# Fixed task lists for five engines, w_in loaded once and copied on chip, and q and k in four chunks, in a fused attention and gated-MLP block

## The chip, the core and the metric

The kernel runs on one core of a Trainium2 chip. The core's engines run side by side, each through its own list of instructions in order, and wait for each other only through semaphores: TensorE (PE in the profile, its weight loads PEld), VectorE (DVE), ScalarE (ACT), GpSimd (POOL) and SyncE (SP), which here issues transfers alone. The metric is the time of one execution in microseconds (us) on the device.

## What is computed

The input is 2048 tokens of width 448, in bf16. First comes attention with 16 heads of 28, in which each token sees itself and seven earlier ones at a distance of two, then an MLP whose gate is mixed over all tokens by a 2048 x 2048 matrix. Cut to its core:

```python
def _A_ref(x, wqkv, wo):               # S = 2048, D = 448, H = 16, Dh = 28
    W, dil = (8, 2)
    qkv = (x @ wqkv).reshape(B, S, 3, H, Dh).transpose(2, 0, 3, 1, 4)
    q, k, v = (qkv[0], qkv[1], qkv[2])
    idx = pos[:, None] - (jnp.arange(W) * dil)[None, :]
    mask = idx >= 0
    logits = jnp.einsum('bhsd,bhswd->bhsw', q, kg) * Dh ** (-0.5)   # kg, vg: k, v at idx
    attn = _softmax(jnp.where(mask, logits, -1e9), axis=-1)
    o = jnp.einsum('bhsw,bhswd->bhsd', attn, vg)
    return o.transpose(0, 2, 1, 3).reshape(B, S, D) @ wo

def _B_ref(x, w_in, w_sp, b_sp, w_out):   # Fh = 896
    z = _gelu(x @ w_in)
    z1 = z[..., :Fh]
    z2 = _layernorm(z[..., Fh:])
    g = jnp.einsum('ts,bsf->btf', w_sp, z2) + b_sp[None, :, None]
    return (z1 * g) @ w_out

h = x + _A_ref(_layernorm(x), A_wqkv, A_wo)
out = h + _B_ref(_layernorm(h), B_w_in, B_w_sp, B_b_sp, B_w_out)
```

## The kernel before

**Tiling.** The tokens are cut into two halves of 1024 (the streams, s = 0 and 1), which lie in the two halves of the 128 partitions of `xh`, `qT` and `kT`, so that one pair of matmuls with 64 rows each works on both at once. A *unit* u is 128 tokens of each stream (blocks u and u + 8 of `x_tm`); there are eight. An attention *tile* i is 114 tokens of each stream; there are nine. 14 tokens ahead of the second stream (the halo, `xhalo`) are normalized apart.

**Stages.** For each unit: statistics on DVE (`bn1_*`), the reciprocal root on POOL (`rs1_*`, function `rstd`), normalization on DVE (`nrm1_*`), and the transpose into `xh`, by TensorE for units 0 to 2 (`tT1_*`, evicted by `ev1_*`) and by a transposing transfer on SP for units 3 to 7 (`tD1_*`). The weights of q, k and v land in 64 partitions, and copies (`cpq*`, `cpk*`, `cpv10`) bring them to both halves. q and k are made in chunks of tokens (`mmq*`, `mmk*`, L791, evicted by `evq*`, `evk*`), three chunks with borders 0, 128, 512, 1024 for q. Each tile then takes v (`mmv`, L831), logits (`mml`, L866, 64 small matmuls), Exp on ACT (`exp`, L879), a band mask on DVE (`mask`, L886), row sums (`mmr`, L895), Ln and Exp on ACT for the reciprocal (`ln`, `rex`, L903 and L925), outputs (`mmo`, L915, 64 small matmuls) and their scaling on DVE (`ot`, L933). For each unit follow the projection (`mmy`, L969), the residual sum (`h`, L977), the second normalization and transposing transfer (`tD2_*`), and the gated half of w_in (`mmz2`, L989) with Gelu on ACT (`ge`) and its own normalization. Then come the other half (`mmz1`, L1033, Gelu `gz1`), the token mixing (`g`, L1070, 448 matmuls of 512 columns, evicted by `ua` and `um` on DVE) and the last projection (L1099, `oa`, stores `st`).

**What sets the order.** The kernel is written as some 650 tasks with an engine, a duration, dependencies, and claims on pools (eight PSUM banks, rings of buffers). `Planner.run` simulates the engines and, whenever one is free, gives it the ready task of the lowest priority number. Priorities come from a due time per tile (`t_tile`) and the offsets in `OFF`, with random noise from `SEED`. The task's instructions are emitted when it is picked, so that the order of picking is the order of the instructions on each engine. `Sched.issue` turns reads and writes of buffers into semaphore waits. A dependency that touches no buffer orders the simulation only; where a transfer must in fact wait, it stands in `waits`.

**Warm-up.** `c_warm` (L616) fills the tile `warm` on DVE. Once its task has ended, the planner fills a gap that it foresees on TensorE with matmuls of `warm` by `warm` (`fill`, L633), whose results nobody reads.

**Transfers.** x comes by `ld_x` (L576), the weights of q, k, v by `ld_w` (L583), w_in by `ld_win` (L591): each half of its columns is read twice from memory, once for each half of the partitions, on ACT's queue. w_sp comes in 32 transposing transfers on SP (`ld_wsp`, L950), 16 for each half of the output tokens; in each chain one waits until the one before it has landed. All of SP's instructions are in one line, so that a transfer that waits holds the ones behind it.

**Instructions.** TensorE's credit (`QUEUE`, `ISSUE`, `pe_time`) stands for instructions that wait ahead of it: small matmuls cost at least 31 ns each once the credit is used up.

Of the kernel before, what the change touches and what calls it, by code (L numbers as in the profile page):

```python
# [36 lines left out]
MPEN = 68.974  # L37
OFF = {"q": -480.93, "v": 1236.52, "evv": 825.88, "l": -1029.33, "exp": 175.61, "mask": -1046.78, "r": -491.23, "o":
       -1335.49, "ln": 982.35, "ot": 136.39, "y": -146.01, "h": 162.89, "ln2": 571.73, "z2": 105.24, "ge": 2308.87,
       "n3": 1032.57, "x0": -505.85, "xd": 734.44, "evq": 1025.79, "cp": 119.01, "td": 182.58}  # L40
SEED, SIGMA = 242706, 1.0
O_AFTER_LN = True
NBANKS = 8
TU = 29.85
# [128 lines left out]
class Task:  # L173
    __slots__ = ("name", "eng", "dur", "emit", "deps", "prio", "acq", "rel", "mode", "epoch",
                 "gate", "nbytes", "start", "end", "succ", "ndep", "rt", "nmm", "alts", "bw", "waits", "mark")

    def __init__(self, name, eng, dur, emit, deps=(), prio=0.0, acq=(), rel=(), mode=None,
# [14 lines left out]
        self.bw = 215.0  # L192
        self.waits = []
# [8 lines left out]
class Planner:  # L202
# [4 lines left out]
    def __init__(self, pools, epochs, table_task, marker):  # L207
        self.tasks = []
        self.named = {}
        self.filler = None  # L210
        self.marker = marker
        self.rng = random.Random(SEED)
        self.pools = {k: [(0.0, s) for s in v] for k, v in pools.items()}
        self.epochs = epochs
        self.table_task = table_task

    def add(self, *a, **k):
        t = Task(*a, **k)
        if SIGMA and not t.nbytes:
            t.prio += self.rng.gauss(0.0, SIGMA)  # L220
# [21 lines left out]
    QUEUE = 90  # L242
    FILL = (0.5, 0.3, 0.25)
    ISSUE = 0.031
    SWITCH = 0.1

    def pe_time(self, t, credit):

        return max(t.dur, (t.nmm - credit) * self.ISSUE)

    def run(self, setup=2.0, t0=0.7):
        import heapq
        tasks = self.tasks
        for t in tasks:
            for d in t.deps:
                d.succ.append(t)
            t.ndep = len(t.deps)
# [17 lines left out]
        credit, credit_at = float(self.QUEUE), 0.0  # L275
# [5 lines left out]
        while ndone < len(tasks):  # L281
# [22 lines left out]
            while progress:  # L304
                progress = False
                for e in self.ENGS:
# [3 lines left out]
                    cr = min(self.QUEUE, credit + (now - credit_at) / self.ISSUE)  # L310

                    def key(t):
                        if e != "pe":
                            return t.prio
                        return t.prio + (MPEN if t.mode != pe_mode else 0.0) + WPEN * (self.pe_time(t, cr) - t.dur)
                    best = None
                    for t in sorted(ready[e], key=key):
                        if t.rt > now + 1e-9:
                            continue
                        if t.epoch is not None and t.epoch > cur:  # L320
# [22 lines left out]
                    if t.epoch is not None:  # L343
                        want = self.epochs[t.epoch]
                        if loaded != want:
                            self.table_task(want)
                            loaded = want
                            extra += 1.3
                        left[t.epoch] -= 1
# [4 lines left out]
                    if e == "pe":  # L354
                        dur = self.pe_time(t, cr)
# [3 lines left out]
                        credit = max(0.0, cr - t.nmm + (dur + extra) / self.ISSUE)  # L359
                        credit_at = now + dur + extra  # L360
                        credit = min(credit, self.QUEUE)
                    if e == "pe" and self.filler is not None and self.pools["ps"]:
                        tf, bank = min(self.pools["ps"])
                        room = now - max(free["pe"], tf + 0.3, self.filler[0].end + 0.2) - self.FILL[1]
                        if room > self.FILL[0]:
                            self.filler[1](bank, int(room / self.FILL[2]) + 1)
# [3 lines left out]
                    if t.nbytes:  # L370
                        beg = max(dma_free, now + 0.3)
                        dma_free = beg + t.nbytes / t.bw / 1000.0
                        t.end = dma_free + setup
# [18 lines left out]
def bass_sequential_preLN__sliding_local_dilated__mixer_gmlp__prompt_kernel(  # L392
# [18 lines left out]
    with contextlib.ExitStack() as top:  # L411
# [25 lines left out]
        nhalf = sb("nhalf", [128, 2], F32)  # L437
        st1 = sb("st1", [128, NB, 6], F32)
# [54 lines left out]
        r_win = [[Res("w_in%d_%d" % (z, s)) for s in range(2)] for z in range(2)]  # L493
        r_q = [[Res("q%d_%d" % (c, g)) for g in range(4)] for c in range(3)]
        r_k = [[Res("k%d_%d" % (c, g)) for g in range(4)] for c in range(3)]
# [17 lines left out]
        r_nhalf = Res("nhalf")  # L513
        r_ln1 = [Res("ln1_%d" % b) for b in range(NB)]
# [41 lines left out]
        def dma(eng, name, fn, nbytes, deps=(), prio=0.0, reads=(), writes=(), rel=(), store=False, issue=0.5, bw=245.0, after=()):  # L556
# [13 lines left out]
            t.bw = bw  # L570
            return t
# [15 lines left out]
        t_win = {}  # L587

        def ld_win(z, prio):
# [17 lines left out]
        t_x[2].deps.append(t_x[8])  # L607
        t_x[2].waits.append(t_x[8])
# [8 lines left out]
        cst("c_nhalf", [(lambda e: e.memset(nhalf[:], -0.5), [], [r_nhalf])], 0.1, prio=-99.5)  # L617
# [30 lines left out]
        def ln_unit(u, which, src_deps, prio, ev_deps):  # L648
# [8 lines left out]

            def em_r():
                rr = [rl[bl[0]], rl[bl[1]]]
                rstd(rs[:, u:u + 9:8], mv[:, u:u + 9:8, 1], nhalf[:, 0:2], rr)  # L660
            tr = add("rs%d_%d" % (which, u), "pool", 1.1, em_r, deps=tb, prio=prio)
# [9 lines left out]
            if u in DMA_T[which]:  # L671
# [3 lines left out]
                    rel=[("tr", h)], issue=1.3)  # L675
# [20 lines left out]
        for u in range(NU):  # L696
            t_xh.append(ln_unit(u, 1, [t_x[u], t_x[u + 8]], OFF["x0"] + OFF["xd"] * u, ()))
            if u == 0:
# [6 lines left out]
                th = add("rsh", "pool", 1.05, lambda: rstd(rsh[:, :], mvh[:, 1:2], nhalf[0:16, 0:1], [r_lnh]), deps=[th], prio=2.2)  # L705
# [45 lines left out]
        for n, (p, h, j) in enumerate([("q", h, j) for j in range(2) for h in range(2)] +  # L751
# [4 lines left out]
            def em(p=p, h=h, j=j, tk=tk):  # L756
                if p == "v":
                    copy(tk[0].eng, wv[64:128], wv[0:64], [r_st[p]], [r_w[p][1]])
                else:
# [3 lines left out]
                    prio=OFF["cp"] + 0.1 * n, alts={"dve": dve4x(ne), "act": act_c(ne)})  # L763
# [3 lines left out]
        CQ = [0, 128, 512, ST]  # L767
        CK = [0, 128, 526, ST + HALO]
        t_q = [[None] * 4 for _ in range(3)]
        t_k = [[None] * 4 for _ in range(3)]  # L770
        qk_all = []
        for ch in range(3):
# [395 lines left out]
```

## Time and profile before

| | |
|---|---|
| time, median of 3 runs | 257.35 us (256.37 to 263.96) |
| the profiled execution's own time | 257.56 us |
| its span, first to last instruction | 255.5 us |
| mean granted TensorE clock | 0.987 |
| TensorE matmuls, weight loads | 2915, 2927 |
| moved by transfers | 21.63 MB |

The span is the part of an execution between the first and the last recorded instruction; the 2.06 us between span and time lie around it. "Busy" counts an engine's time in compute instructions. The profile's chain goes back from the last instruction: at each step to what released it, or to the instruction before it on its engine; "issue" is time in which the engine waited for nothing that the profile shows. Here 38% of the chain is L1070, the token mixing, and 87% is TensorE.

### The profile page before, as it was taken

The numbers are of one execution on the slowest core, as the hardware profiler recorded it, in microseconds if no ns is written. First come the engines' busy times: TensorE is split into PE (matmuls) and PEld (weight loads), VectorE is DVE, ScalarE is ACT, GpSimd is POOL, SyncE is SP. The second block draws the span as 40 slices with busy tenths as digits, with TensorE's granted clock in tenths as the row PEclk, the third lists the DMA queues.
The fourth block names the chain that finished last, engine by engine and source line by source line (L and its number), as shares of the span: only waits on it lengthen the run. The fifth ranks groups of instructions, "written<-read, shape, count | busy, mean of one in ns | idle before, by whom it ended". The sixth has DMA issues, their size and how long they took to land.

```text
span 255.5 us, 6474 instructions
## 1 busy us (share of the span) xinstructions
PE 243.1 (95%) x2915; PEld 119.2 (47%) x2927; DVE 146.4 (57%) x282; ACT 86.6 (34%) x93; POOL 29.9 (12%) x74
## 2 busy tenths in 40 slices
PE   7979999699898999999999999999999999999995
PEld 2555564245454455444454444454444444454442
DVE  6879955558899699998036532252234333342333
ACT  2796647553697556666671000000000000000000
POOL 5622210000221114222002000000000000000000
PEclk9999999799999799999999999999999999999999
DMA  6962459979494989994345333010000200011002
GB/s 156 245 143 41 58 93 153 175 162 176 93 105 79 176 128 188 164 176 94 67 82 85 82 82 82 3 54 18 0 3 0 72 0 3 0 36 37 0 3 72
DMA packets 55332, 21.63 MB, mean 85 GB/s; under 512 B 46584, under 2 KB 55176, under 8 KB 55304
## 3 DMA queue, kind: packets, MB, share of 16 engines
q1 hardware_dynamic: 51624, 16.45, 34.9%
q10 hardware_dynamic: 3680, 4.76, 9.7%
q8 instruction: 23, 0.38, 0.6%
q14 instruction: 5, 0.04, 0.1%
HBM read 7.99 MB, written 1.84 MB: 38 GB/s over the span
## 4 chain that ended last, share of the span: by engine, by line
PE 87%; DMA 4%; DVE 3%; issue 2%; ACTq 1%; ACT 1%
PE psum L1070 38%; PE psum L791 9%; PE psum L989 8%; PE psum L1099 8%; PE psum L1033 8%; PE psum L831 5%; PE psum L969 5%; DMA reg<-in_A_wqkv_dram 4%; PE psum L915 2%; PE psum L866 1%; PE psum L895 1%; DVE x_tm L977 1%; DVE reg L641 1%; ACT reg L879 1%; ACTq L576 1%
## 5 line engine op out<-in xcount | busy, mean ns | idle before, releaser
L1080 DVE TENSOR_TENSOR ub<-psum,reg 128x512 bf16<-128x512 f32 x28 | 19.4, 692 | 62.3 <-PE psum L1070 62.3
L1070 PE MATMUL psum<-reg,z2p 128*128 128x512 bf16 x218 | 48.5, 379 | 0.3
L1070 PE MATMUL psum<-wspT_lo,z2p 128*128 128x512 bf16 x219 | 48.2, 379 | 0.4 <-issue 0.2
L1070 PEld LDWEIGHTS psum<-wspT_lo,z2p 128*128 128x128 bf16 x224 | 21.7, 98 | 26.7 <-DVE ub L1080 0.4
L1070 PEld LDWEIGHTS psum<-reg,z2p 128*128 128x128 bf16 x224 | 21.9, 98 | 26.3
L791 PE MATMUL psum<-xh,reg 64*128 64x128 bf16 (+3 forms) x336 | 27.4, 316 | 0.6 <-ACT reg L639 0.6
L1005 DVE BATCH_NORM_STATS2 st<-z2p 128x6 f32<-128x448 bf16 x32 | 17.7, 609 | 10.6 <-ACT z2p L999 10.6
L989 PE MATMUL psum<-w_in,xh 64*128 64x448 bf16 x224 | 22.0, 350 | 0.0
L1099 PE MATMUL psum<-reg 128*128 128x448 bf16 x112 | 21.8, 353 | 0.0
L1033 PE MATMUL psum<-xh,w_in 64*128 64x512 bf16 x196 | 21.5, 377 | 0.0
L654 DVE BATCH_NORM_STATS2 st<-x_tm 128x6 f32<-128x448 bf16 x32 | 19.4, 608 | 0.5 <-DMA x_tm<-in_A_x_dram 0.5
L791 PEld LDWEIGHTS psum<-xh,reg 64*128 64x128 bf16 x336 | 13.9, 96 | 12.6 <-issue 3.6
L879 ACT ACTIVATE reg<-psum 128x928 bf16<-128x928 f32 x18 | 15.9, 945 | 11.3 <-PE psum L866 11.3
L639 ACT ACTIVATE reg<-psum 128x896 bf16<-128x896 f32 (+4 forms) x18 | 14.6, 833 | 11.6 <-PE psum L791 6.0
L644 POOL TENSOR_SCALAR rs<-mv 128x2 f32<-128x2 f32 x24 | 6.2, 259 | 104.9 <-DVE mv L655 75.5
L645 POOL TENSOR_TENSOR rs<-rs,nhalf 128x2 f32<-128x2 f32 x24 | 18.2, 759 | 2.0
L999 ACT ACTIVATE z2p<-psum 128x896 bf16<-128x896 f32 x16 | 14.6, 917 | 8.1 <-PE psum L989 8.1
L1043 ACT ACTIVATE reg<-psum 128x1024 bf16<-128x1024 f32 x14 | 14.3, 1023 | 7.0 <-PE psum L1033 7.0
L641 DVE CAST reg<-psum 128x1024 bf16<-128x1024 f32 (+3 forms) x11 | 12.5, 1132 | 7.0 <-PE psum L791 6.3
L1099 PEld LDWEIGHTS psum<-reg 128*128 128x128 bf16 x112 | 10.9, 98 | 10.5
L989 PEld LDWEIGHTS psum<-w_in,xh 64*128 64x128 bf16 x224 | 10.6, 94 | 10.5 <-issue 0.6
L831 PE MATMUL psum<-reg,xh 64*64 64x448 bf16 x252 | 15.0, 378 | 0.4 <-ACT reg L879 0.3
(62 smaller groups left out, 205.0 us busy)
## 6 DMA issues: line engine op xcount, KB each, us to landing
w_in<-in_B_w_in_dram ACTq DMA_DIRECT2D x4, 784.0 KB, 8.2
out_dram<-tring SPq DMA_DIRECT2D x16, 112.0 KB, 1.7
x_tm<-in_A_x_dram SPq DMA_DIRECT2D x13, 112.0 KB, 8.4
z2p<-in_A_wqkv_dram ACTq DMA_DIRECT2D x2, 392.0 KB, 7.5
reg<-in_B_w_out_dram SPq DMA_DIRECT2D x1, 784.0 KB, 6.7
reg<-in_B_b_sp_dram SPq DMA_DIRECT2D x1, 512.0 KB, 4.0
reg<-in_A_wqkv_dram ACTq DMA_DIRECT2D x1, 392.0 KB, 11.1
reg<-in_A_wo_dram SPq DMA_DIRECT2D x4, 98.0 KB
```

The lines of the kernel that those rows point to most:

```text
L641: iss(eng, lambda e: e.tensor_copy(dst, src), reads=rd, writes=wr)
L645: iss("pool", lambda e: e.tensor_tensor(dst, dst, nh, ALU.pow), reads=rr + [r_nhalf], writes=rr)
L654: iss("dve", lambda e: e.bn_stats(st[:, b, :], x_tm[:, b, :]), reads=[r_x[b]], writes=[rl[b]])
L791: iss("pe", lambda e, c=c, s=s, gi=gi, lhs=lhs: e.matmul(psum[:, bk[s] * 512 + cw * gi:bk[s] * 512 + cw * gi + cw], lhs, xh[64 * s:64 * s ...
L831: iss("pe", lambda e, c=c, s=s, w=w: e.matmul(psum[64 * w:64 * w + 64, bk[s] * 512:bk[s] * 512 + D], xh[64 * s:64 * s + 64, c, HX - HALO + ...
L879: iss("act", lambda e: e.activation(E[:, es[0], 2 * n:2 * n + 2, :], pair_view(lb, 0, 8 * JW), AF.Exp, scale=SCALE), reads=[r_bank[lb[0]], ...
L989: iss("pe", lambda e, c=c, s=s: e.matmul(psum[:, zb[s] * 512:zb[s] * 512 + D], xh[64 * s:64 * s + 64, c, HX + 128 * u:HX + 128 * u + 128], ...
L1005: iss("dve", lambda e, b=b: e.bn_stats(st3[:, b, k, :], z2p[:, b, D * k:D * k + D]), reads=[r_z2[b][k]], writes=[r_st3[b][k]])
L1033: iss("pe", lambda e, c=c, s=s: e.matmul(psum[:, bk[s] * 512:bk[s] * 512 + 512], w_in[64 * s:64 * s + 64, c, 128 * f:128 * f + 128], xh[64 ...
L1070: iss("pe", lambda e, b=b: e.matmul(psum[:, gb[0] * 512:gb[0] * 512 + 512], z2p[:, b, 128 * f:128 * f + 128], src[:, b, 512 * (tc % 2):512 ...
L1080: iss("dve", lambda e: e.tensor_tensor(ub[:, us_[0], :], psum[:, gb[0] * 512:gb[0] * 512 + 512], bb[:, 512 * tc:512 * tc + 512], ALU.add), ...
L1099: iss("pe", lambda e, f=f: e.matmul(psum[:, wb[0] * 512:wb[0] * 512 + D], z1p[f][:, 128 * m:128 * m + 128], w_out[:, f, :], start=(f == 0) ...
```

## The change

1. **Lists in place of a search at build time.** `SEQ` holds, for SP, POOL, DVE, ACT and TensorE in this order, the numbers of all 667 tasks, counted as they are made. `Planner.replay` walks these lists and takes at each step the head task that can start first; where a task may run on either of two engines, the list says which. Only the choice of PSUM banks and ring buffers, the table loads and the warm-up matmuls still hang on the simulated times. `OFF`, `TU` and `MPEN` get other numbers, and the noise goes.
2. **Instruction packets.** `fetch` takes the place of the credit: TensorE's instructions come in packets of 256 (two for each matmul), a packet is asked for when TensorE is 115 past the packet before, is needed 320 later, and takes some 2.5 us once the transfers under way have landed.
3. **w_in once.** Each half of the columns is read once, in two pieces of four and three row groups, on SP's queue, into the lower 64 partitions. Four copies (`cpw`) bring it to the upper 64.
4. **q and k in four chunks**, borders 0, 128, 256, 512, 1024 for q. Two groups of heads share a pair of banks up to 256 columns.
5. **Smaller edits.** A task `c_tab` with no work makes ACT load the table set of Exp and Ln at the start. `rs1_*` may run on ACT as Ln and Exp instead of POOL. All loads of x for units 2 to 7, not the first alone, wait for x8.

```diff
+CHUNK, ASK, NEED = 256, 115, 435
+FETCH = (0.95, 2.5)
...
+            if a < b:
+                t = now + shift + dur * max(0, a - n) / m
+                free = max(t + self.FETCH[0], self.landed - 0.3, free)
+                new.append(free + self.FETCH[1])
+                free += 1.1
+                ka += 1
...
-            for s in range(2):
-                t_win.setdefault(z, []).append(dma("act", "win%d_%d" % (z, s), lambda e, s=s: e.dma_start(
-                    w_in[64 * s:64 * s + 64, :, FH * z:FH * z + FH],
-                    B_w_in[:, FH * z:FH * z + FH].rearrange("(c p) n -> p c n", p=64)),
-                    D * FH * 2, prio=prio + 0.01 * s, writes=[r_win[z][s]], bw=330.0))
+            for n, (c0, c1) in enumerate(C4):
+                def view(s, c0=c0, c1=c1):
+                    return w_in[64 * s:64 * s + 64, c0:c1, FH * z:FH * z + FH]
+                t = dma("sp", "win%d_%d" % (z, n), lambda e, v=view, c0=c0, c1=c1: e.dma_start(
+                    v(0), B_w_in[64 * c0:64 * c1, FH * z:FH * z + FH].rearrange("(c p) n -> p c n", p=64)),
+                    64 * (c1 - c0) * FH * 2, prio=prio + 0.01 * n, writes=[r_win[z][0][n]], bw=200.0)
...
+                def em(v=view, n=n, tk=tk):
+                    copy(tk[0].eng, v(1), v(0), [r_win[z][0][n]], [r_win[z][1][n]])
...
+                if tk[0].eng == "pool":
+                    rstd(dst, var, nhalf[:, 0:2], rr)
+                else:
+                    iss("act", lambda e: e.activation(dst, var, AF.Ln, bias=epst[:, 0:1]), reads=rr + [r_eps], writes=rr)
+                    iss("act", lambda e: e.activation(dst, dst, AF.Exp, scale=-0.5), reads=rr, writes=rr)
...
-        CQ = [0, 128, 512, ST]
-        CK = [0, 128, 526, ST + HALO]
+        CQ = [0, 128, 256, 512, ST]
+        CK = [0, 128, 270, 526, ST + HALO]
...
-                per = 512 // cw if ch else 2
+                per = 2 if cw <= 256 else 1
```

The lists, with the names of their tasks in place of the numbers, in the stretches that matter:

- SP: x0 xhalo x4 x3 x10 x7 x6 x2 x5 x11 wo2 x12 x13 x15 tD1_3 x14 wo3 win1_0 tD1_4 tD1_7 tD1_6 tD1_5 wsp0_0 wsp0_8 win1_1 wsp0_1 wo0 wsp0_9 wo1 win0_0 wsp0_2 wsp0_10 wsp0_3 tD2_2 tD2_1 wsp0_11 wsp0_4 win0_1 wsp0_12 tD2_3 tD2_0 w_out ...
- ACT: x1 x8 x9 wk wq c_tab rs1_0 cpk00 cpq00 ev1_1 ev1_0 evq1_0 wv evk1_0 cpq01 evq0_0 evk1_2 evk0_0 evq0_2 evk0_2 evq1_2 ev1_2 exp0 exp0 evv1 rs1_7 exp1 exp1 evv2 evv0 ln0 rs1_6 ln1 evq2_0 rex0 rex1 evq2_2 evv3 exp2 exp2 exp3 exp3 ln2 evq3_0 cpw1_1 rex2 ln3 evk3_2 evk3_3 rex3 exp4 ... rex8 ge2_1 ge2_0 cpw0_0 ge1_1 ...
- DVE: c_th0 c_wo0 bn1_0 bn1_1 bn1_8 bn1_9 nrm1_0 bnh nrm1_8 nrm1_1 nrm1_9 cpq10 nrmh cpk01 cpk10 cpq11 evh ... ot1 evq3_1 mask2 evq3_3 mask3 evk3_1 evk3_0 cpw1_0 ot2 ... nrm2_5 cpw0_1 ... um3_3 ua3_5 c_warm oa10 ...
- TensorE: tT1_0 tT1_1 tTh mmq1_0 mmk1_0 mmq0_0 mmk0_0 mmk1_2 mmq0_2 mmk0_2 mmq1_2 tT1_2 mml0 mmv1 mmv0 mml1 mmv2 mmq2_0 mmr0 mmr1 mmq2_2 mmk2_2 mmk2_0 mmo0 mmv3 mmo1 mml2 mmq3_1 mmq3_3 mml3 mmq3_0 mmr2 mmk3_1 mmo2 mmr3 mmo2 mmk3_0 mmk3_3 mmk3_2 mmq3_2 mmv6 mmo3 mml4 mmo3 mmy1 mml5 mmv4 mmr4 mmy2 mmv5 mmo4 mmr5 mmo4 mml6 mmy0 mmo5 mml6 mmv8 mml7 mmy3 mmr6 mmy4 mmo6 mmr7 mmo6 mml8 mmv7 mmy5 mmr8 mmo7 mmz2 ...

More of the change, by code (lines that the diff above doesn't have):

```diff
@@ L241, with fetch @@
     SAME = {"pe": 0.0, "act": 0.09, "dve": 0.08, "pool": 0.0, "sp": 0.0}
-    QUEUE = 90
     FILL = (0.5, 0.3, 0.25)
-    ISSUE = 0.031
     SWITCH = 0.1
-    def pe_time(self, t, credit):
-        return max(t.dur, (t.nmm - credit) * self.ISSUE)
-    def run(self, setup=2.0, t0=0.7):
+    CHUNK, ASK, NEED = 256, 115, 435
+    FETCH = (0.95, 2.5)
+    def fetch(self, nmm, now, dur, commit=False):
+        n, m = self.pe_n, 2 * nmm
+        ka, kn, free, av, shift = self.k_ask, self.k_need, self.f_free, self.avail, 0.0
+        new = []
+        while True:
+            a, b = self.CHUNK * ka + self.ASK, self.CHUNK * kn + self.NEED
+            if min(a, b) > n + m:
+                break
+            if a < b:
[5 more added lines that the diff above has]
+            else:
+                t = now + shift + dur * max(0, b - n) / m
+                v = av[kn] if kn < len(av) else new[kn - len(av)]
+                shift += max(0.0, v - t)
+                kn += 1
+        if commit:
+            self.pe_n, self.k_ask, self.k_need, self.f_free = n + m, ka, kn, free
+            av.extend(new)
+        return shift
@@ new lines, in slots @@
+    def slots(self, p, n, t):
+        free = {s: f for f, s in self.pools[p]}
+        if len(free) < n:
+            return None
+        if p != "ps":
+            s = min(free, key=lambda s: (free[s], s))
+            return max(t, free[s]), [s]
+        if n == 2:
+            pairs = [(max(free[b], free[b + 1]), b) for b in range(0, NBANKS, 2) if b in free and b + 1 in free]
+            if not pairs:
+                return None
+            f, b = min(pairs)
+            return max(t, f), [b, b + 1]
+        t = max(t, min(free.values()))
+        now = [s for s in sorted(free) if free[s] <= t]
+        alone = [s for s in now if free.get(s ^ 1, 1e18) > t]
+        return t, [min(alone or now, key=lambda s: free[s])]
@@ L252, in run @@
+    def run(self, t0=0.7):
+        if SEQ:
+            return self.replay()
         import heapq
         tasks = self.tasks
+        for t, a in zip(tasks, ADJ):
+            t.prio += a
         for t in tasks:
@@ L319, in run @@
                             continue
-                        if t.epoch is not None and t.epoch > cur:
+                        if e == "act" and t.epoch is not None and t.epoch > cur:
                             continue
@@ L342, in run @@
                     extra = 0.0
-                    if t.epoch is not None:
+                    if t.epoch is not None and e == "act":
                         want = self.epochs[t.epoch]
@@ L354, in run @@
                     if e == "pe":
-                        dur = self.pe_time(t, cr)
+                        if t.nmm:
+                            dur = t.dur + self.fetch(t.nmm, now, t.dur, True)
                         if t.mode != pe_mode:
@@ L365, in run @@
                         if room > self.FILL[0]:
-                            self.filler[1](bank, int(room / self.FILL[2]) + 1)
+                            nf = int(room / self.FILL[2]) + 1
+                            self.fetch(nf, now - room, room, True)
+                            self.filler[1](bank, nf)
                     t.start = now
@@ L554, in dve4x, with dma @@
             return (190.0 + 0.26 * n) / 1000.0
-        def dma(eng, name, fn, nbytes, deps=(), prio=0.0, reads=(), writes=(), rel=(), store=False, issue=0.5, bw=245.0, after=()):
+        def dma(eng, name, fn, nbytes, deps=(), prio=0.0, reads=(), writes=(), rel=(), store=False, issue=0.5, bw=245.0, after=(), setup=2.0):
             def em():
@@ L606, in bass_sequential_preLN__sliding_local_dilated__mixer_gmlp__prompt_kernel @@
             ld_x(u + 8, 0.1 + 0.01 * u + 0.001)
-        t_x[2].deps.append(t_x[8])
-        t_x[2].waits.append(t_x[8])
+        for u in range(2, NU):
+            for b in (u, u + 8):
+                t_x[b].deps.append(t_x[8])
+                t_x[b].waits.append(t_x[8])
+        add("c_tab", "act", 0.01, lambda: None, prio=-18.5, epoch=0)
         def cst(name, fns, dur, eng="pool", prio=0.0, deps=()):
@@ L815, in chunks @@
         def chunks(cb, lo, hi):
-            return [c for c in range(3) if cb[c] < hi and (c == 2 or cb[c + 1] > lo)]
+            return [c for c in range(NCH) if cb[c] < hi and (c == NCH - 1 or cb[c + 1] > lo)]
         t_v = []
@@ L951, in ld_wsp @@
                 dst[:, b, :], B_w_sp[1024 * half:1024 * half + 1024, 128 * b:128 * b + 128], transpose=True),
[L952 removed]
+                128 * 1024 * 2, prio=prio, deps=deps, writes=[r_wsp[b][half]], after=extra, issue=1.2, bw=165.0, setup=1.25)
         S_ORDER = [b for u in range(NU) for b in (u, u + 8)]
```

164 lines of the change are left out of this document (124 added, 40 removed), and 30 rows, old and new, of the table SEQ.

## The prediction

> **What bounds the kernel now.** I read the page, then the chain that ended last, then the busy time by stretches, then the timelines of TensorE, ACT and the queues. The page first:
>
> ```profile
> span 255.5 us, 6474 instructions
> ...
> PE 243.1 (95%) x2915; PEld 119.2 (47%) x2927; DVE 146.4 (57%) x282; ACT 86.6 (34%) x93; POOL 29.9 (12%) x74
> ...
> PEclk9999999799999799999999999999999999999999
> ...
> q8 instruction: 23, 0.38, 0.6%
> ```
>
> TensorE is busy for 95% of the span, no other engine for more than 57%, and twice the granted clock falls to 7 tenths. So a gain can only come from TensorE's gaps, from its slow stretches, or from its late start. Where these lie is told by the stretches (columns: length, then busy time and count of PE, PEld, DVE, ACT, POOL; granted clock; DMA share; GB/s):
>
> ```profile
> 9.80:94.66 84.86, 77.53 (x1951) 42.48 (x1951) 67.06 (x116) 55.85 (x63) 13.43 (x26) 0.96 0.74 126
> 22.80:94.66 71.86, 66.16 (x1681) 34.93 (x1682) 55.56 (x87) 44.47 (x50) 9.16 (x16) 0.95 0.77 124
> 94.66:252.63 157.97, 157.28 (x942) 73.54 (x952) 72.53 (x153) 27.16 (x28) 10.24 (x22) 1.00 0.28 56
> 44.94:48.35 3.41, 0.89 (x68) 0.67 (x64) 1.85 (x2) 1.75 (x2) 0.00 (x0) 1.00 1.08 196
> 48.35:51.77 3.42, 3.42 (x40) 1.28 (x35) 1.13 (x1) 1.78 (x2) 0.00 (x0) 0.50 1.05 139
> 82.49:85.90 3.41, 3.41 (x36) 1.38 (x31) 2.55 (x6) 1.48 (x2) 0.92 (x2) 0.50 0.91 118
> ```
>
> From 94.66 to the last matmul TensorE has no gap: 157.28 of 157.97 us. Nothing in the change shortens the work there, so those 158 us stay, and so do the 2.84 us of add and store behind it (252.63 to the span's end). All that can move lies before 94.66. The chain shows what is there:
>
> ```profile
> 3.73 11.14 DMA reg<-in_A_wqkv_dram
> ...
> 21.55 1.24 PE psum L633 x5
> ...
> 46.35 1.85 issue
> ...
> 49.13 4.44 PE psum L791 x28
> ...
> 56.70 3.13 PE psum L791 x28
> ...
> 66.04 0.29 issue
> ...
> 67.02 1.45 PE psum L831 x28
> ...
> 69.42 0.73 issue
> ...
> 81.28 0.89 issue
> ...
> 82.55 2.76 PE psum L831 x28
> ...
> 252.66 0.62 DVE tring L1107
> ```
>
> TensorE's useful work before 94.66: 77.53 busy from 9.80 on, less 2.3 us of warm-up matmuls (the 1.24 us row, and 1.04 us at 10.89, whose row stands with the start below), less what the half clock added. The two half-clock stretches added 3.2 us: 28 matmuls of L791 took 4.44 instead of 3.13, the 28 of L831 took 2.76 instead of 1.45, and their neighbours some 0.5. That leaves 72.0 us, so 22.7 us of the first 94.66 are loss. By 22.8 us (77.53 - 66.16 - 2.3) 9.1 us of work were done, so the start lost 13.7 us. The other 8.9 are 5.7 us of idle time (71.86 - 66.16) and the 3.2 of half clock. Of the idle 5.7, the four "issue" rows are 3.76; the rest, 1.9, are short waits for ACT and DVE.
>
> **The start, step by step.** These rows carry it:
>
> ```profile
> 1.50:7.40 5.90, 5.90 (x14) 2.09 (x15) 3.38 (x8) 1.28 (x1) 3.59 (x13) 1.00 0.90 215
> 7.42 2.04 PEld L633 LDWEIGHTS psum<-warm 128*128 128x128 bf16 x10 [0.25 <-issue]
> 7.46 3.03 ACT L639 ACTIVATE reg<-z2p 64x1568 bf16<-64x1568 bf16 x2 [1.61 <-DMA z2p<-in_A_wqkv_dram]
> 10.89 1.04 PE L633 MATMUL psum<-warm 128*128 128x512 bf16 x4
> 11.96 3.04 ACT L639 ACTIVATE reg<-z2p 64x1568 bf16<-64x1568 bf16 x2 [0.66 <-DMA z2p<-in_A_wqkv_dram]
> 11.87 2.61 PE L791 MATMUL psum<-xh,reg 64*128 64x128 bf16 x85
> 15.03 2.06 ACT L639 ACTIVATE reg<-psum 128x512 bf16<-128x512 f32 x4
> L639 ACT ACTIVATE xh<-psum 128x896 bf16<-128x896 bf16 x2 | 1.9, 931 | 0.0
> ```
>
> Before: the q weights land at 7.46, the k weights at 11.96, v's at 14.87 (3.73 + 11.14). The first real q matmul is at 11.87, on a full clock, because warm-up matmuls ran from 1.50. They took 421 ns each until 7.40 (14 in 5.90) and 204 ns after (10 in 2.04): the clock was half for 5.9 us, although no clock record covers that stretch.
>
> After, read from the task lists: the numbers are places in the order in which tasks are made. Task 21, the memset of `warm`, stands near the end of the DVE list, and the filler asks for its end. So **no warm-up matmul is left** at the start. ACT issues x1, x8, x9, wk, wq, and wv only after its first q eviction. Ahead of the second weight stand the same five transfers on ACT's queue as before (three of 112 KB, two of 392), so I expect it near 11.6, a little earlier because v's no longer share the queue. Bounds: 12.0, as before, and 9.9, if SP's later start (its loads wait for x8, now second) frees the engines. Between 7.46 and 11.96 ACT's queue moved 616 KB in 4.5 us, 137 KB/us.
>
> On ACT the copy `cpq00` waits for that weight (1.51 us, to 13.1), and behind it stand the evictions of the transposes (0.93 each). So the first q matmul goes at 14.1 instead of 11.87. Then TensorE has eight groups of 28: 128 (or 142) columns, chunks 0 and 1. 85 matmuls took 2.61, so 28 take 0.86, the eight 7.0. At half clock for 5.1 us (the middle of a 3.4 us stretch, the shortest seen, and two of these) 2.55 us are lost; bounds 1.7, and 2.95 from the 5.9 us. ACT's own work meanwhile (eight evictions of 0.52, `cpq01` 1.51, wv's issue 0.76, one eviction of 0.93) ends by 23, so TensorE is what ends last. The first logits, `mml0`, start at 14.1 + 7.0 + 2.55 + 0.5 (a transpose) = 24.2, with 9.2 us of work done: 15.0 us lost, **1.3 more than before**.
>
> The clock has a page. The Trainium skill, "TensorE: Matmul & The Clock Gate", Part 1, says that half rate is the resting state and is lifted after about 3.4 us of sustained work, and that an idle window brings it back. The rows agree with the second half (0.89 us busy in 3.41, then 3.42 at 0.50); for the start they show 5.9 us. By the page's 3.4 the loss would be 1.7 and the sum 0.85 lower. It speaks against the change, which drops the warm-up.
>
> **The parts of the change.** The rows they use:
>
> ```profile
> L791 PE MATMUL psum<-xh,reg 64*128 64x398 bf16 x56 | 5.2, 329 | 0.0
> L791 PE MATMUL psum<-xh,reg 64*128 64x384 bf16 x56 | 4.9, 323 | 0.0
> L641 DVE COPY reg<-reg 64x3136 bf16<-64x3136 bf16 x1 | 1.0, 971 | 1.2 <-DMA reg<-in_A_wqkv_dram 1.2
> L644 POOL TENSOR_SCALAR rs<-mv 128x2 f32<-128x2 f32 x24 | 6.2, 259 | 104.9 <-DVE mv L655 75.5
> L645 POOL TENSOR_TENSOR rs<-rs,nhalf 128x2 f32<-128x2 f32 x24 | 18.2, 759 | 2.0
> 19.33 1.28 ACT L531 ACT_TABLE_LOAD   x1
> reg<-in_B_w_sp_dram SPq DMA_TRANSPOSE x16, 3.2
> ```
> - q and k in four chunks: chunk 1 of 398 and 384 columns took 10.1 for 112 matmuls, 9.2 without the overlap of their ends (167 and 161 ns a pair). Now 56 of 128, 56 of 128 or 142, and 112 of 256: 3.6 + 6.2 (an estimate: 111 ns a pair, on the line between 61 for 128 and 167 for 398) against 9.2. **+0.6 us** of TensorE work, 112 matmuls more. Tile 1 no longer waits for units 2 and 3.
> - w_in once and copied. ACT loses four issues, SP gains four. The copies are 64x3584 on DVE (`cpw1_0`), 64x2688 on ACT (`cpw1_1`), 64x3584 on ACT (`cpw0_0`), 64x2688 on DVE (`cpw0_1`). From 0.97 us for 3136 on DVE and 1.51 for 1568 on ACT: 1.1, 2.6, 3.5, 0.9. On the path I cost them at nothing: z2's first matmul lies about 30 us behind `cpw1_1`, and ACT is busy 44 of 72 us after 22.8. SP's four issues (0.6 each) and their bytes stand ahead of w_sp transposes and of wo0 and wo1, which the first y group needs: from 3.2 us a transpose wo1 lands near 52, y starts at 57. If that cover goes, `cpw1_1` costs 2.6 and the wait for its load (third rival).
> - Half the w_in bytes: 1.6 MB less while the transposes of w_sp run. Nothing on the path by itself.
> - The reciprocal root of three units moves from POOL (0.26 + 0.76 us) to two small ACT operations, whose price no row shows; between 0 and POOL's 1.0 each way. The first lies ahead of the second weight, the others in ACT's slack. Nothing.
> - One table set from the start: a 1.28 us table load at 19.33 goes if copies run from that set. It lies in the start's ACT work, which has slack. Nothing; bound -1.28.
> - Fixed lists, with instruction packets modelled. The page has 23 packets and 0.38 MB on the instruction queue, 16 KB each, for 5842 PE and PEld instructions, 254 per packet, and the four "issue" gaps fall inside or just ahead of bursts of small matmuls. The new list puts a q, k, v or y group (1.45 to 1.6 us) between most bursts of logits and outputs. I followed it by hand from 24.2 with the rows' durations, PSUM banks included. TensorE is at `mml1` at 27.8, `mmq2_0` 30.0, `mmo0` 36.6, `mml2` 39.3, `mml3` 43.0, `mmk3_0` 48.0, `mml4` 55.9, the first y at 57.1, and z2 begins near 80; each group finds its banks free and its operands ready, ACT about a microsecond ahead. The closest are `mml3` (its bank free at 42.0) and the transposes of units 5 and 6 for `mmq3_1` at 40 (landing 39). I leave a quarter of the issue gaps, 0.9, and half of the short waits, 1.0. The half clock followed each time a stretch with little work; I leave none. Bounds: all 8.9 as now, and 0. **Loss after the start 1.9 instead of 8.9: -7.0.**
> - The late stage: order changed, work equal, TensorE without gaps. Followed the same way, the last first-half w_sp lands about 117 and is needed at 129; w_sp's second half (3.2 us each) is done near 150 and first used at 174. Nothing.
>
> The page "Runtime: NRT & Kernel Launch" of the Trainium skill, "Instruction fetch mechanics", says that crossing a 256-instruction block costs little and is mostly hidden. If so the 1.85 us gap is no fetch, and spacing the bursts out wins nothing; the first rival carries this.
>
> **Sum.** The profiled execution took 257.56 us (0.2 over the median of 257.35), 2.06 us around its span of 255.5. 257.56 + 1.3 (start) + 0.6 (chunks) - 7.0 = 252.5.
>
> **Rivals.**
> 1. *The gaps stay.* Issue gaps of 3.76 and both half-clock stretches remain, only the waits halve: 257.56 + 1.9 - 1.0 = 258.5; with half of the gaps, 255.0. For it: fetches need a free DMA engine, and the first 40 us are still full of transfers. Against: 1.6 MB fewer bytes. Chance 0.25.
> 2. *The start is early.* The second weight lands at 9.9 (1.7 earlier) and the slow clock costs 1.7 instead of 2.55: 252.5 - 2.5 = 250.0. For it: wv no longer competes. Against: ACT's queue moved 137 KB/us whatever stood behind. Chance 0.18.
> 3. *ACT waits in its line.* `cpw1_1` needs win1_1, which on SP stands behind `tD1_5` and two w_sp transposes, each waiting for the one before:
> ```profile
> 37.03 35.97 SPq L950 DMA_TRANSPOSE wspT_lo<-in_B_w_sp_dram x7
> w_in<-in_B_w_in_dram ACTq DMA_DIRECT2D x4, 784.0 KB, 8.2
> ```
> At 5.1 us each (7 in 35.97), from 36.7, win1_1 goes out at 47 and lands by 55.2; ACT comes to the copy at about 47.5. Exp, Ln and evictions stand behind it, so TensorE runs dry, 7.7 us, and a slow stretch of 1.7 follows: 261.9, slower. It decides once the wait passes 5 us. Against: the 5.1 was with w_in on a second queue; alone w_sp takes 3.2, and win1_1 lands in time. Chance 0.09.
> 4. The forecast, 0.48, by itself 250 to 255.
>
> **Chances.** About 2% is what a measurement of this kernel can tell from no change: below 252.2 is faster, above 262.5 slower. Faster: half of the forecast and most of rival 2, 0.43. Slower: part of rival 3 and what I do not see, 0.07. Within: 0.50. The range 248 to 258 leaves out rival 3, the end of rival 1 and an early start with a fast clock on top.
>
> **What would show it.** The start: no L633 work before 14 us, the second weight's copies near 11.6, the first 64x128 matmuls at over 110 ns a pair. The list: issue gaps before 90 us under 1.5 together, no stretch at 0.50 after 24. The copies: ACT without a wait on w_in. The end: TensorE without gaps from about 25 on and the last attention matmul near 89 instead of 94.66. The forecast is wrong if `mml0` starts after 27 or if the loss behind it exceeds 5 us.

## The result, and the profile after

| | before | after |
|---|---|---|
| time, median of 4 runs each | 257.86 us | 248.05 us (246.72 to 249.34) |
| ratio to before, 95% interval | 1 | 0.964 (0.956 to 0.972) |
| the profiled execution's own time | 257.56 us | 249.34 us |

The change makes the kernel faster by 3.6%. One of the four runs of the kernel before, 263.96 us, was in a slower state; the ratios, and the times of the experiments below (medians), leave such runs out. The time lies 4.5 us below the forecast and only 0.05 us above the lower end of the forecast range, 248. The page of the changed kernel, with the same lines as before:

```profile
span 247.4 us, 6649 instructions
...
PE 232.1 (94%) x3004; PEld 123.7 (50%) x3004; DVE 143.3 (58%) x281; ACT 91.4 (37%) x103; POOL 28.8 (12%) x69
...
q8 instruction: 23, 0.38, 0.7%
```

TensorE is busy 11 us less with 89 matmuls more: the 10.7 us of warm-up matmuls are gone. (What the half clock no longer adds later, 3.2 us, and what it now adds at the start, 2.4, nearly cancel.) The start, from the timelines of ACT and TensorE:

```profile
10.01 1.51 ACT L803 ACTIVATE reg<-z2p 64x1568 bf16<-64x1568 bf16 x1 [0.80 <-DMA z2p<-in_A_wqkv_dram]
...
12.38 9.04 PE L965 MATMUL psum<-xh,reg 64*128 64x128 bf16 x224 [0.82 <-ACT xh L803]
...
21.84 0.72 PE L1040 MATMUL psum<-reg 32*64 32x58 bf16 x64
...
30.42 0.94 PE L965 MATMUL psum<-xh,reg 64*128 64x256 bf16 x14 [1.74 <-issue]
```

L965 is the q and k matmul (L791 before), L1040 the logits (L866 before). The second weight's copy starts at 10.01, the eight groups of q and k run from 12.38 for 9.04 us, and `mml0` starts at 21.84, not at 24.2. Behind it (columns as in the stretches of before; no clock record was left in this execution, so its granted clock reads 1.00, in the start too, where the matmuls themselves show the half clock):

```profile
21.84:244.57 222.73, 220.57 (x2754) 112.87 (x2752) 125.15 (x238) 79.36 (x88) 16.90 (x34) 1.00 0.39 75
```

From the first logits to the last matmul TensorE is idle for 2.2 of 222.73 us; 1.74 of these are the issue gap at 28.68, and 0.27 a second one at 39.91. The kernel before lost 8.9 us in that stage.

So the 8.2 us between the two profiled executions are made up like this: 6.7 are idle time and half clock gone behind the start (8.9 less 2.2), 1.1 are the start (13.7 us lost before, 21.84 - 9.2 = 12.6 now), and 0.4 are left for the rounding of these and for all else, the chunks among it.

### The profile page after: what moved, and what is told of

Same layout as the page of the kernel before. It is cut to its first block, busy times and chain, and to the rows that moved or that the text cites. A ratio compares the mean times of both kernels' runs of the same rounds, so it can differ in the third digit from the quotient of the medians.

```text
span 247.4 us, 6649 instructions
## 1 busy us (share of the span) xinstructions
PE 232.1 (94%) x3004; PEld 123.7 (50%) x3004; DVE 143.3 (58%) x281; ACT 91.4 (37%) x103; POOL 28.8 (12%) x69
## 4 chain that ended last, share of the span: by engine, by line
PE 93%; DMA 3%; issue 1%; ACT 1%; ACTq 1%; DVE 0%
PE psum L1244 39%; PE psum L965 11%; PE psum L1163 9%; PE psum L1273 9%; PE psum L1207 9%; PE psum L1005 5%; PE psum L1143 5%; DMA z2p<-in_A_wqkv_dram 3%; PE psum L1040 3%; PE psum L1089 2%; PE psum L1069 1%; ACT reg L803 1%; ACTq L723 1%; ACT xh L803 0%; ACTq L730 0%
## 5 line engine op out<-in xcount | busy, mean ns | idle before, releaser
L1244 PE MATMUL psum<-reg,z2p 128*128 128x512 bf16 x224 | 50.0, 379 | 0.0
L1244 PE MATMUL psum<-wspT_lo,z2p 128*128 128x512 bf16 x224 | 49.0, 379 | 0.0
L1244 PEld LDWEIGHTS psum<-wspT_lo,z2p 128*128 128x128 bf16 x224 | 21.8, 98 | 26.6 <-issue 0.4
L965 PE MATMUL psum<-xh,reg 64*128 64x128 bf16 (+3 forms) x448 | 28.5, 290 | 2.8 <-issue 2.0
L965 PEld LDWEIGHTS psum<-xh,reg 64*128 64x128 bf16 x448 | 19.4, 105 | 10.5 <-issue 3.4
L1207 PE MATMUL psum<-xh,w_in 64*128 64x512 bf16 x196 | 22.2, 376 | 0.0
L803 ACT ACTIVATE reg<-psum 128x896 bf16<-128x896 f32 (+3 forms) x21 | 16.8, 824 | 5.8 <-PE psum L965 4.2
L1281 DVE TENSOR_TENSOR tring<-psum,x_tm 128x448 bf16<-128x448 f32 x16 | 9.6, 616 | 14.0 <-PE psum L1273 14.0
L1163 PEld LDWEIGHTS psum<-w_in,xh 64*128 64x128 bf16 x224 | 11.9, 94 | 9.5 <-issue 0.9
L1217 ACT ACTIVATE reg<-psum 128x1024 bf16<-128x1024 f32 x14 | 13.7, 1030 | 7.8 <-PE psum L1207 7.8
L1207 PEld LDWEIGHTS psum<-xh,w_in 64*128 64x128 bf16 x196 | 11.1, 94 | 9.7
L809 POOL TENSOR_TENSOR rs<-rs,nhalf 128x2 f32<-128x2 f32 x21 | 15.6, 743 | 1.8
```

Of the source, the lines that this page charges most:

```text
L803: iss("act", lambda e: e.activation(dst, src, AF.Copy), reads=rd, writes=wr)
L809: iss("pool", lambda e: e.tensor_tensor(dst, dst, nh, ALU.pow), reads=rr + [r_nhalf], writes=rr)
L965: iss("pe", lambda e, c=c, s=s, gi=gi, lhs=lhs: e.matmul(psum[:, bk[s] * 512 + cw * gi:bk[s] * 512 + cw * gi + cw], lhs, xh[64 * s:64 * s ...
L1163: iss("pe", lambda e, c=c, s=s: e.matmul(psum[:, zb[s] * 512:zb[s] * 512 + D], xh[64 * s:64 * s + 64, c, HX + 128 * u:HX + 128 * u + 128], ...
L1207: iss("pe", lambda e, c=c, s=s: e.matmul(psum[:, bk[s] * 512:bk[s] * 512 + 512], w_in[64 * s:64 * s + 64, c, 128 * f:128 * f + 128], xh[64 ...
L1244: iss("pe", lambda e, b=b: e.matmul(psum[:, gb[0] * 512:gb[0] * 512 + 512], z2p[:, b, 128 * f:128 * f + 128], src[:, b, 512 * (tc % 2):512 ...
```

## The experiments

Eleven runs follow, one of them the changed kernel again, in three groups, each group on one chip together with runs of the kernel before. Ratios are to that kernel on the same chip.

**The start: what brought the weights early.** The first kernel lets the loads of x go at once, as before:

```diff
             for b in (u, u + 8):
-                t_x[b].deps.append(t_x[8])
-                t_x[b].waits.append(t_x[8])
+                if b == 2:
+                    t_x[b].deps.append(t_x[8])
+                    t_x[b].waits.append(t_x[8])
```

> The changed kernel, but of the loads of x for units 2 to 7 only x2 waits for x8, as before. Theory (the gate): with all of them held back, the weights of k and q have the DMA engines alone from 4 to 7 us, and that is why the second weight was there at 10.0 instead of the 11.6 forecast. Then here its copy on ACT starts at 11 to 12 us, the first q matmul follows 2.4 us behind, mml0 starts 1 to 2 us later than its 21.84, and the time is 1 to 2 us above 248.05. Rival (v's weights moved behind the first q eviction are the reason): the copy still starts at 10.0, mml0 at 21.8, time 248.

The second moves `wv` on ACT's list from behind `evq1_0` to behind `wq`.

> The changed kernel, but ACT issues the load of v's weights right behind those of k and q. Theory (the gate): v's weights stand behind the others in the same queue and take nothing from them; the second weight's copy starts at 10.0 to 10.4, mml0 within 0.5 us of 21.84, time 247.5 to 248.5. Rival (the late v is the reason): the copy starts at 11 to 12 us, mml0 at 23 to 24, time 249 to 250.

Without the hold on x the time is 249.64 us, ratio 0.979 (0.973 to 0.986); with v's weights early it is 247.02, ratio 0.968 (0.963 to 0.973). The second weight's copy and the first logits, first with x let go, then with v early:

```profile
11.18 1.51 ACT L804 ACTIVATE reg<-z2p 64x1568 bf16<-64x1568 bf16 x1 [0.98 <-DMA z2p<-in_A_wqkv_dram]
...
22.79 0.70 PE L1041 MATMUL psum<-reg 32*64 32x58 bf16 x64
```
```profile
9.54 1.51 ACT L778 ACTIVATE reg<-z2p 64x1568 bf16<-64x1568 bf16 x1 [0.61 <-DMA z2p<-in_A_wqkv_dram]
...
20.83 0.70 PE L1015 MATMUL psum<-reg 32*64 32x58 bf16 x64
```

The bytes whose transfer began between 3 and 7 us, by queue, from the records of the transfers:

```
KB from 3 to 7 us      SP's queue   ACT's queue
before                     287          613
changed kernel               2          816
x let go                   333          550
v early                      1          792
```

The hold on x is the reason: it gives the weights the engines alone for 4 us. The place of v's weights is not. The copy is 1.2 us later with x let go than in the profile above and 1.6 later than with v early, the logits 1.0 and 2.0 us, and beside the kernel with v early on the same chip the time is 2.6 us longer, somewhat more than the logits alone explain. In the nine other profiles in which x is held and the lists stand, this copy starts at 9.23 to 9.84.

**The missing warm-up.** `c_warm` goes to the head of DVE's list; the planner then puts 26 warm-up matmuls ahead of the first transposes.

```diff
-    (25, 29, 31, 43, ...
+    (21, 25, 29, 31, 43, ...
```

> The changed kernel with the memset of warm at the head of DVE's list, so that the planner puts 26 warm-up matmuls ahead of the first transposes. Theory: the 224 q and k matmuls that ran from 12.38 for 9.04 us, half of that time at 107 ns a pair, take 6.4 to 7.2 us here, mml0 starts near 19.8 to 20.5, and the time falls by 1.3 to 2.3 us to about 246. Rival (the copies and evictions on ACT bound that stretch, not the clock): the matmuls run at 56 ns a pair but with gaps, mml0 stays at 21.3 to 22, time 248. A second rival: the warm-up matmuls run past 7.5 us and hold the transposes back, so that the first q matmul comes after 13 us and the gain is lost.

It gave 248.98 us, ratio 0.975 (0.968 to 0.982): not faster than the changed kernel (0.964). Neither rival is the reason, as the timeline and TensorE's waits between 20 and 95 us show:

```profile
12.18 6.61 PE L940 MATMUL psum<-xh,reg 64*128 64x128 bf16 x224 [0.85 <-ACT xh L778]
...
19.21 0.70 PE L1015 MATMUL psum<-reg 32*64 32x58 bf16 x64
```
```profile
PE psum L940 <- issue: 1.5, 2, 1.0
PE psum L980 <- issue: 1.2, 1, 1.2
PE psum L1064 <- issue: 1.0, 2, 0.6
```

The start did what the theory said: the same 224 matmuls take 6.61 us instead of 9.04, and the logits come 2.6 us earlier. But 3.7 us of waits for instructions, in five places, stand behind it, where the changed kernel has 2.0. That gives back 1.7 of the 2.6. In its second profile (below) the changed kernel itself started the logits at 20.74 and waited 2.1 us; beside that one all of the gain is given back. The next question was why.

**One whole packet of warm-up.** 128 warm-up matmuls of 64 columns are 256 instructions, so that every packet border stands against the same later instruction as without them.

```diff
-            for _ in range(n):
+            for _ in range(128):
                 iss("pe", lambda e: e.matmul(
-                    psum[:, bank * 512:bank * 512 + 512], warm[:, 0:128], warm[:, :]),
+                    psum[:, bank * 512:bank * 512 + 64], warm[:, 0:128], warm[:, 0:64]),
```

> The changed kernel with the memset of warm first on DVE, and 128 warm-up matmuls of 64 columns, 256 instructions, one whole packet, ahead of the first transposes. With 26 of 512 columns mml0 came 2.6 us earlier, but issue gaps of 0.5 to 1.2 us in six places gave all of it back. Theory (the gaps came because the packets' borders had moved by 52 instructions against the bursts that the list was made for): with a whole packet the borders stand as in the changed kernel, the gaps behind 22 us sum to less than 2 us, mml0 at 19 to 20, and the time falls to about 245.5 to 246.5. Rival (TensorE that is 2.6 us earlier runs into packets that come no earlier, wherever the borders are): gaps of 3 to 4 us in sum, time 248 to 249.5. If 64 columns do not lift the clock, the 224 q and k matmuls take 8.5 to 9.4 us again and nothing is won.

Its yardstick, the changed kernel again on the same chip:

> The changed kernel itself, as the yardstick for the runs beside it: 246.7 to 249.3 us, mml0 near 21.8, one issue gap of over 1 us before 40 us or none, since which packet comes late hangs on a few tenths of a microsecond.

The changed kernel took 247.96 us, ratio 0.969 (0.961 to 0.976), with waits for instructions of 2.1 us in four places; the gap of 1.74 us at 28.68 was 0.64 here. Its logits came at 20.74, not near 21.8 as expected: its second weight's copy started at 9.23 instead of 10.01, and its q and k matmuls took 8.72 us instead of 9.04. So the start of one and the same kernel differs by 1.1 us between these two profiles:

```profile
20.74 0.70 PE L1040 MATMUL psum<-reg 32*64 32x58 bf16 x64
```

With the packet of warm-up it took 246.57, ratio 0.964 (0.957 to 0.971). The first two lines are its stretches around the first q matmul, the third all of TensorE's waits between 20 and 95 us:

```profile
9.00:11.74 2.74, 0.33 (x7) 0.24 (x8) 2.33 (x5) 2.37 (x3) 2.40 (x6) 1.00 1.10 338
12.83:16.24 3.41, 3.41 (x70) 3.41 (x66) 3.21 (x8) 2.56 (x4) 1.81 (x7) 0.50 0.54 130
```
```profile
PE psum L1044 <- issue: 0.4, 1, 0.4
```

The waits fell to 0.4. The clock was won only in part: after the idle 9.0 to 11.74 it fell to half once more, and `mml0` came at 20.41 instead of the 19 to 20 expected, only 0.3 us ahead of the yardstick. So of the 2.8 us between the two profiled executions (248.27 and 245.45) 1.7 are the waits. The medians lie 1.4 us apart, and their intervals overlap.

**Whole packet or not.** To tell the borders from the mere earliness of TensorE, 154 warm-up matmuls of 52 columns: nearly as long, but 308 instructions.

> The changed kernel with 154 warm-up matmuls of 52 columns at the start: as long as the 128 of 64, but 308 instructions, one packet and 52 more. Theory (the lists fit the packets' borders, and a shift of 52 instructions breaks the fit): the issue gaps between 20 and 80 us come back to 2.5 to 5 us, against 0.4 in the profile with 128, and the time is 1 to 3 us above 246.6. Rival (where the borders fall does not matter; the gaps with 26 warm-up matmuls came from TensorE being early): gaps and time as with 128, within 0.7 us.

It gave 249.25 us, ratio 0.971 (0.966 to 0.977), 2.7 us above the kernel with 128 (the two ran on different chips), and 3.2 above the kernel of the next experiment, which ran beside it. Its waits in the same stage:

```profile
PE psum L940 <- issue: 1.1, 1, 1.1
PE psum L1064 <- issue: 0.9, 2, 0.7
PE psum L980 <- issue: 0.8, 1, 0.8
```

2.8 us against 0.4. Its logits came at 19.13, 1.3 us earlier than with 128, close to the 19.21 of the 26 warm-up matmuls, which are also 52 instructions. The theory's forecast came, both in waits and in time. Earliness is not fully excluded: these two kernels are also the two earliest. Among five kernels whose borders stand unmoved, though, an earlier start did not go with more waiting: logits at 22.79 (x let go) and 1.7 us of waits, 21.84 and 2.0, 20.83 (v early) and 0.9, 20.74 and 2.1, 20.41 and 0.4.

That the gaps are waits at packet borders can be read from the traces' records directly. Count TensorE's matmuls and weight loads in order in each of the thirteen profiles (before, after and these eleven). Between 12 and 130 us there are 35 waits for instructions of 0.29 us or more. In all 35 the first matmul behind the wait stands 177 to 194 instructions past a multiple of 256, and it starts 2.2 to 3.4 us (in 34 of them 2.2 to 3.0) after the transfer of an instruction packet began.

**Filling the idle time.** The 128 in three places: 64 of 128 columns ahead of `tT1_0`, 44 of 64 ahead of `tTh`, 20 of 64 ahead of `mmq1_0`.

> The changed kernel with 128 warm-up matmuls, one packet in all, laid by hand into TensorE's idle time: 64 of 128 columns ahead of the first transposes, 44 of 64 columns behind them, 20 of 64 ahead of the first q matmul. With all 128 at the start the clock fell to half again at 12.8 us, just as the q matmuls began, for 3.4 us. Theory: with the idle 9.0 to 11.7 us filled, the 224 q and k matmuls take 6.4 to 7 us instead of 8.24, mml0 starts at 18.7 to 19.5, the issue gaps behind it stay under 2 us in sum, and the time is 245 to 246. Rival: TensorE, earlier still, meets packets and transfers that come no earlier; gaps of 2 to 3 us, time as with all 128 at the start (246.6).

246.06 us, ratio 0.959 (0.955 to 0.963), the lowest of all, and the same as with all 128 at the start within the intervals. The clock stays full, but the time won is lost again at once:

```profile
12.03 6.00 PE L940 MATMUL psum<-xh,reg 64*128 64x128 bf16 x202 [0.16 <-ACT xh L778]
...
19.25 0.79 PE L940 MATMUL psum<-xh,reg 64*128 64x128 bf16 x22 [1.22 <-issue]
...
20.46 0.70 PE L1015 MATMUL psum<-reg 32*64 32x58 bf16 x64
```

TensorE waits 1.22 us for instructions in the last q group, and the logits start at 20.46. That is the rival's effect, ahead of the logits: a TensorE that is early runs into its packet, whose transfer began at 16.63. Behind the logits no wait for instructions is left. With v's weights early on top:

> As the one with 128 warm-up matmuls in three places, with the load of v's weights right behind those of k and q as well, which alone made no difference. Both theories: within 0.7 us of that kernel; if v's weights held the attention up once TensorE is earlier, 0.5 to 1 us less.

247.22 us, ratio 0.967 (0.960 to 0.974). The wait in the q groups is 1.86 us there, at 14.20, and the logits start at 20.93. The time is 1.2 us above the kernel without the move, more than the 0.7 that both theories allowed; there is no gain.

**A transfer moved.** `win1_0` stands on SP behind `tD1_5` instead of behind `wo3`.

> The changed kernel with the first load of w_in moved on SP behind the last transposing transfer of the first normalization (from 24.0 to about 36 us). Theory (an instruction packet waits for transfers under way): the packet that started at 27.61, some 270 instructions later than the quiet stage asks, starts 1.5 to 3 us earlier, the issue gap of 1.74 us at 28.68 shrinks below 0.7, and if no other gap comes in its place the time falls by about 1 us. Rival (the packet is late for another reason, such as the burst of 64 + 56 + 64 + 28 small matmuls alone): the gap stays at 1.5 to 1.9 and the time at 248. The copy on ACT may come to wait for the second load, up to 2 us, since that too moves back.

The gap at 28.68 is gone, and by the transfers' records the packet that had started at 27.61 starts at 24.29. That much is the theory's. It fits that with v early, where `win1_0` stands unmoved, the same packet starts at 23.51, just ahead of that load's issue at 23.54, and the gap is missing there too. But the time is 250.66 us, ratio 0.982 (0.976 to 0.988). The chain now runs through the second w_in load and its copy on ACT:

```profile
34.69 6.81 DMA wspT_lo<-in_B_w_sp_dram
...
42.74 5.46 DMA w_in<-in_B_w_in_dram
...
48.22 2.44 ACT w_in L778
...
58.79 1.51 issue
```

This is the forecast's third rival at work, on a small scale: ACT waits 1.85 us for the load, and TensorE 0.8 us for what stands behind the copy. In the changed kernel the same copy starts at 47.91 without a wait. The rest of the loss lies elsewhere: two new waits for instructions, 1.0 us at 40.88 and the 1.51 at 58.79, and behind the latter a stretch at half clock, from 61.98 to 65.40, on which TensorE lost 1.7:

```profile
61.98:65.40 3.42, 3.42 (x26) 1.05 (x19) 1.12 (x1) 2.62 (x4) 0.00 (x0) 0.50 0.89 58
```

**w_in from memory twice.** The copies are left out, and a second transfer on SP fills the upper partitions.

```diff
+                def both(em0=t.emit, v=view, c0=c0, c1=c1, n=n):
+                    em0()
+                    iss("sp", lambda e: e.dma_start(v(1), B_w_in[...]),
+                        writes=[r_win[z][1][n]], prod="dma", inc=16)
+                t.emit = both
...
-                    copy(tk[0].eng, v(1), v(0), [r_win[z][0][n]], [r_win[z][1][n]])
+                    pass
```

> The changed kernel, but both halves of the partitions get w_in from memory, as before, the second transfer right behind the first on SP, and the four copies on chip are left out. Theory (half the bytes win nothing by themselves; they only free queues): between the first logits and z2 no new gap of over 0.5 us, ACT and DVE have 8 us less to do, time within 1 us of the changed kernel's. Rival (the transfers hold back instruction packets and the w_sp chain): two or more issue gaps of 0.5 to 2 us between 22 and 60, time 1.5 to 4 us longer.

253.04 us, ratio 0.987 (0.979 to 0.996), 5.1 us above the changed kernel on the same chip, more than the 1.5 to 4 of the rival. Its chain:

```profile
28.08 1.46 issue
...
47.35 1.01 issue
...
59.66 1.63 issue
...
87.03 5.41 DMA xh<-tring
```

There are three gaps of over 1 us, as the rival said, the first of which the changed kernel has too (1.74 and 0.64 in its two profiles), and later a transposing transfer of the second normalization that the longer line on SP brings late. TensorE's waits for instructions behind the logits sum to 4.7 us against 2.1 in the yardstick; for the late transfer it waits 0.6. Part of the loss is therefore packets, but whether the bytes delay them or the place of the loads on SP is not separated. The test is harsher than the kernel before, whose w_in loads were on ACT's queue.

**The lists.** The planner with the new offsets and packets, and `SEQ = ()`.

> The changed kernel without its lists: the planner picks the order by priorities again, with the new offsets and packets in its model, w_in once, four chunks, the x loads held back, and 25 warm-up matmuls come back. Theory (the lists carry what is won behind 22.8 us): idle time and half clock between 22 us and the first gapless stretch are 5 to 9 us, as in the kernel before, and the time is 251 to 256. Rival (the packets in the model or the fewer bytes carry it): that loss is below 3 us, and the time within 1.5 us of the changed kernel's.

262.06 us, ratio 1.024 (1.017 to 1.032): 14.1 us above the changed kernel and slower than the kernel before. The stretch from 20 to 95 us, first with the lists (the changed kernel on the same chip), then without:

```profile
20.00:95.00 75.00, 72.82 (x1916) 42.04 (x1912) 61.32 (x98) 57.87 (x65) 5.88 (x15) 1.00 0.66 107
```
```profile
20.00:95.00 75.00, 64.06 (x1683) 36.50 (x1679) 59.80 (x94) 50.25 (x52) 10.62 (x19) 0.95 0.62 103
```

Without the lists TensorE is idle for 10.9 of 75 us and falls to half clock twice; with them it is idle for 2.2. The loss is larger than the 5 to 9 us expected. So the rival, that the packets in the model or the fewer bytes carry the gain without the lists, is excluded. The 14 us are not the lists' price in general: these offsets were not chosen for use without them.

## Why the prediction came out as it did

The forecast, 252.5, lay just inside the 2% that it counted as no change. It gave 0.43 to the kernel being faster by more than that, as it is, and 0.50 to its staying within.

*The stage behind the first logits* was right in place and size: a loss of 1.9 us was forecast, and 2.2 were measured. Its make-up was not as forecast: 0.9 of waits for instructions and 1.0 of short waits for other engines were left in, and 2.0 of the first and 0.15 of the second came. So the sum agrees in part by luck. No stretch fell to half clock (the groups of 28 v matmuls between 26 and 78 us took 1.45 to 1.52 us each, where one took 2.76 at half clock before; the clock record of the changed kernel's second profile reads 1.00 from 16 us to the end), and the copies of w_in cost nothing on the path: `cpw1_1` was forecast at 47.5 for 2.6 us and ran at 47.91 for 2.44. The order followed by hand put the first y at 57.1 and z2 near 80; they came at 57.54 and 80.20. That is chance in part: the hand count began at 24.2 and held no loss, the run began 2.4 us earlier and lost 2.2. Of the signs named for this stage, these two did not come: issue gaps under 1.5 together (2.0), and TensorE without gaps from 25 on.

*The start* was the term of the sum that was mis-sized, and its sign was wrong: 1.3 us more loss than before were forecast, and 1.1 less came. The step reads "I expect it near 11.6", of the second weight, with 9.9 as the early bound. It came by 10.0, since the hold on x left 816 KB instead of 613 to ACT's queue between 3 and 7 us. The prediction took its rate, 137 KB/us, from a kernel in which x's loads shared the engines from the start. The right reason stood beside the bound ("if SP's later start ... frees the engines"); the reason given for a small gain and for the second rival, that v's weights no longer share the queue, is not it, as the kernel with v early shows. The forecast start, 24.2, then came at 21.84: 2.4 of the 3.2 us by which the profiled execution lay below the forecast. Of these 1.7 are the first q matmul (12.38 instead of 14.1), and most of the rest is its work, 6.6 us at full clock instead of 7.0. This is the first half of the second rival, whose 250.0 lies 0.7 us above that execution; its other half, a slow clock that costs 1.7, did not come.

*The clock* was right at the start. 2.55 us of loss were forecast for the missing warm-up; the same matmuls took 9.04 us and, warmed up, 6.61, so 2.43 were lost. (In the five other profiles without warm-up matmuls they took 8.50 to 9.35.) The premise that the half clock "followed each time a stretch with little work" holds for one of the two stretches before. Ahead of the other TensorE had been busy for 2.21 of 3.42 us, mostly with the small matmuls:

```profile
79.07:82.49 3.42, 2.21 (x142) 1.42 (x140) 3.39 (x7) 2.22 (x3) 0.93 (x2) 1.00 0.47 81
```

So little work is not the whole condition, and why no stretch fell later is not shown; that none fell is. What the prediction did not see is that this loss could hardly be won back: a start 2.6 us earlier with 52 instructions more brought nothing.

*The chunks* were costed at +0.6 us of work. Their price alone was not measured, but 224 matmuls at 6.61 us are 59 ns a pair, not the 61 to 67 assumed, so on the 56 pairs of the second chunk about 0.3 of it was not there; the 256-column pairs took 112 ns as estimated (84 matmuls in 4.69 us).

*Half the bytes of w_in* were costed at "nothing on the path by itself". Under these lists loading them twice on SP costs 5.1 us, which speaks against that; how much of it is the bytes and how much SP's longer line stays open.

*The instruction packets.* That the gaps are waits for packets and that the order of the list avoids them was the forecast's ground for -6.0 of its -7.0. The first half is shown by the 35 gaps, all at one place of the packet. For the second, the shifted borders and the order without lists agree with it; that order moves all else too, so the lists' gain is shown as a whole, not its share from packets. The Trainium skill's page "Runtime: NRT & Kernel Launch", "Instruction fetch mechanics", has the cost of a border mostly hidden. That fits most of the 23 or so packets of each kernel here; at one to five of them, in every kernel, TensorE waited 0.29 to 2.35 us.

## What to carry to other kernels

Where all input is asked for at once, hold back the loads that are needed late: the second weight came 1.2 to 2.0 us earlier for a wait laid on the loads of x. When a fixed order of small matmuls runs with few waits at the places where instruction packets end, anything put ahead of it should be tried at the length of a whole packet; 52 instructions more did not pay here. And before an idle engine is sped up, ask which queue has to deliver earlier for it.

## What the runs showed of the hardware that I had not expected

- 52 more instructions ahead of the same list went with waits for instructions of 2.8 and 3.7 us behind the logits; the kernels with none more and w_in loaded as in the changed kernel had 0.9 to 2.1, those with 256 more 0 to 0.7.
- All 35 waits for instructions of 0.29 us or more stand 177 to 194 instructions past a multiple of 256.
- 128 warm-up matmuls of only 64 columns lift the clock as 26 of 512 do; there, with 0.33 us of work in the 2.74 us before 11.74, it fell again at 12.83 for 3.41 us.
- Some 0.33 MB of loads on one queue took 266 KB from another in the same 4 us (816 against 550).
